# Two q/k pairs between the halves of W_out, and the next batch's V on the ACT queue: a fused attention and hard-swish kernel on one core

## The chip, the cores and the metric

The kernel runs on one core of one Trainium2 chip. The metric is the device time of one execution in microseconds (us); less is better. All times below are in us unless they say otherwise.

## What is computed

Causal attention with a window of 64 positions (8 batches, 8 heads, 576 positions, head size 64), then a two-layer feed-forward block over the 4608 resulting rows. Inputs and output are float32.

```python
scores = q @ k.T / sqrt(64)                      # per batch and head
mask = (i - j >= 0) & (i - j < 64)
attn = softmax(where(mask, scores, -1e9))
x = (attn @ v) put together to [4608, 512]
h = x @ w_in                                     # [512, 2048]
g = h * clip(h + 3, 0, 6) / 6
out = g @ w_out                                  # [2048, 512]
```

## The kernel before

The feed-forward block works on nine blocks of 512 rows, T = 0 to 8. For each block, `s1(T)` multiplies with W_in (64 matmuls of 512 columns, tile `ps`, L769); ACT makes relu(h/6 + 1/2) of every two blocks of 128 columns (`relu`, tile `t`, L778), and DVE limits that to 1 and multiplies it with h (`gT`, L781). Then `s2(T)` multiplies with W_out (64 matmuls, tile `acc`, L813) and ACT copies each of the four accumulators out (`osb`, L830), which SP stores. Between the matmuls of `s2(T)` stand the units of attention of batch T + 1: T (transposes on TensorE, L570, for batches 0 and 1 only), S (scores, L601 or L650, followed by an exponential on ACT and a mask on DVE, L621 or L660), PV (attention times V, L674, L687 and L692, followed by a normalisation on DVE, L712 and L715) and X (transposes of the result, L739; from batch 2 on a DMA transpose, L722). Each unit serves one of four groups of two heads. Three pairs of PSUM banks serve all of `ps`; two accumulators serve `acc`.

The kernel builds its own order: a planner (`Plan`) holds a heap of operations with assumed durations, and every engine's instructions come out in the order of the planned starts. At run time each engine and each queue works strictly in that order and waits on semaphores.

Loads arrive in staging tiles (six of `st`, three of `tl` for the short last piece) and are cast to bf16. Batches 0 and 1 load q and k as four pairs, one for each group (L337, tile `runs`), whose casts go to DVE, ACT or POOL, whichever the planner finds free first. Batches from 2 on load q and k "naturally" in five pieces each (L463, tile `nat`), cast by POOL, and transposed by one DMA each on SP (L442, tile `QKT`). V comes in five pieces. For batches 0 and 1 it is on SP (L420, L362); from batch 2 on, `stream_v` issues it on ACT's queue (L389), and POOL makes up to three casts of each piece, one into `V` and two into a copy shifted by 64 rows, which lies in the memory of `runs`. The first full-width weights are four blocks of W_in (L493; the first in two halves) and four of W_out (L508), cast by POOL.

SP takes the loads in the order that `load_items` yields. For batch 0 and batch 1 `MERGE` says how q/k pairs (p) and pieces of V (v) alternate:

```python
MERGE = ('ppppvvvppvpvpvvvvv', "ppppppvpvpvvv")
```

so that the order is batch 0, all of W_in, all of W_out, batch 1 with V among the last pairs, and then q and k of batch 2, 3 and so on. `stream_v(b)` is put into the plan after q and k of batch b; its issues depend on `("pv", b - 2, NG - 1)` and `("issued", b, 0)`, that is, on the last PV of batch b - 2 and on the issue of the q transpose of batch b.

All DMAs issued by SP and ACT take one of eight semaphores in turn, in the order of the program. Each issue waits until the DMA that last used its semaphore, eight issues before, has landed.

`s2(0)` takes its 64 matmuls in an order of its own, since W_out is still arriving: block columns 0 to 11 for the first two groups of 128 rows, then 12 to 15 for these, then the other two groups.

Of the kernel before, what the change touches and what calls it, by code (L numbers as in the profile page):

```python
# [21 lines left out]
NQT = 1  # L22
NPT = 3
VGAP = 1.8
VRATE = 150
NXP = 2
NEG = -30000.0
QK_ENG = ((('DVE', 'ACT'), ('ACT',), ('ACT',), ('ACT',)), (("DVE", "ACT"),) * 4)
MERGE = ('ppppvvvppvpvpvvvvv', "ppppppvpvpvvv")
ORDER = (('T', 0), ('T', 1), ('S0', 0), ('S1', 0), ('S1', 1), ('T', 2), ('S0', 1), ('PV', 0), ('S1', 2), ('T', 3), ('S0', 2), ('PV', 1), ('S1', 3), ('PV', 2), ('S0', 3), ('X', 0), ('PV', 3), ('X', 2), ('X', 1), ('X', 3))  # L30
X_ENG = ((('DVE',), ('DVE', 'ACT'), ('DVE',), ('DVE', 'ACT')), (("DVE", "ACT"),) * 4)
NWARM = 11
# [71 lines left out]
def kernel(  # L104
# [10 lines left out]
    P = nc.NUM_PARTITIONS  # L115
    B, H, S, D = q.shape
    DM, FF = moe_w_in.shape
    NT = B * S
    NG = H // 2
# [5 lines left out]
    NFC = FF // P  # L125
# [171 lines left out]

    def load_items():

        for b in range(B):  # L300
            if b < NR6:
                ps, vs = load_pairs(b), load_v_halves(b) if b == 0 else load_v(b)
                for c in MERGE[b]:
                    yield next(ps if c == "p" else vs)
            else:
                yield from load_nat(b)
            if b == 0:
                yield from load_w()

    def casts(key, land, pieces):  # L310

# [14 lines left out]
    def load_pairs(b):  # L326

        for gg in range(0, NG, 2):
            tiles = {}
            deps = [stage_slot([("cast", b, i, gg), ("cast", b, i, gg + 1)]) for i in range(2)]  # L330
            for g in (gg, gg + 1):
                for i, src in enumerate((q, k)):
                    def go(s, g=g, i=i, src=src, tiles=tiles):
                        if i not in tiles:
                            tiles[i] = stage.tile([P, 2, R * D], F32, name="st", tag="st")
                        st = tiles[i][:, g % 2, :]
                        nc.sync.dma_start(  # L337
                            out=st,
                            in_=src[b, 2 * g : 2 * g + 2].rearrange("h (p j) d -> (h p) (j d)", j=R),
                        )  # L340
                        fr, land = moved(s, 295, 385 if b else 330)
                        casts(("cast", b, i, g), land, [
                            (("DVE", "ACT", "POOL"), runs[i][b * NG + g][:], st.rearrange("p (j d) -> p j d", j=R), R * D)])
                        return fr
                    yield b, deps[i], go
# [27 lines left out]
    def stream_v(b):  # L373

        V, W = V_ring[b % 2], W_ring[b % 2]
        tiles = {}
        deps = stage_slot([("cast", b, 2, i) for i in range(KB - 1)]) + (("pv", b - 2, NG - 1), ("issued", b, 0))
        tdeps = tail_slot([("cast", b, 2, KB - 1)])

        def issue(kb):  # L380
            ss = min(P, S - kb * P)
            def fn(s):
                if kb == 0:
                    tiles["t"] = stage.tile([P, 4, H * D], F32, name="st", tag="st")
                    tiles["l"] = tails.tile([P, H * D], F32, name="tl", tag="tl")
                if kb == KB - 1:
                    pl.mark(("vgo", b), s)
                st = tiles["l"][:ss, :] if kb == KB - 1 else tiles["t"][:, kb, :]
                nc.scalar.dma_start(  # L389
                    out=st.rearrange("p (h d) -> p h d", h=H),  # L390
                    in_=v[b, :, kb * P : kb * P + ss, :].rearrange("h s d -> s h d"),
                )
                dma["v"] = max(dma["v"], s) + 262 * ss / P / VRATE
                land = dma["v"] + 2.7
                sv = st.rearrange("p (g h d) -> p g h d", g=NG, h=2)
                todo = [(("POOL",), W[D:P, :, kb, :, 0:D], sv[0:D], H * D)]
                if ss == P:
                    todo.append((("POOL",), V[:, :, kb, :, 0:D], sv, H * D))
                    todo.append((("POOL",), W[0:D, :, kb + 1, :, 0:D], sv[D:P], H * D))
                casts(("cast", b, 2, kb), land, todo)  # L400
                if kb < KB - 1:
                    pl.op("ACT", s + VGAP, 0.45, issue(kb + 1))
            return fn
        pl.op("ACT", 0.0, 0.45, issue(0), deps=deps + tdeps)

# [23 lines left out]
                yield b, deps + tdeps if kb == KB - 1 else deps, go  # L429

    def load_nat(b):
        for i, src in enumerate((q, k)):
            T = {"left": KB}
            n = natural[i]
            deps = stage_slot([("cast", b, i, j) for j in range(KB - 1)])
            if b > NR6:
                deps += (("vgo", b - 1),)
            if b > NR6:
                deps += (("tr", b - 1, i),)
            def tr(t, i=i, n=n):  # L440
                def fn(s):
                    nc.sync.dma_start_transpose(  # L442
                        out=QK_tiles[b % NQT][:, i * NG : (i + 1) * NG, :].rearrange("d g (k t) -> d (g k) t", t=P),
                        in_=n[:].rearrange("p g k d -> p (g k d)"),
                    )
                    fr, land = moved(s, 655, 230)
                    pl.free["SP"] = fr
                    pl.mark(("issued", b, i), s)
                    return land
                d = (("S", b - NQT, NG - 1),) if b >= NQT else ()  # L450
                if b > 2:
                    d += (("s1", b - 1),)
                pl.op("SP", t, 0.1, fn, ("tr", b, i), deps=d)
            for kb in range(KB):
                ss = min(P, S - kb * P)
                def go(s, i=i, src=src, kb=kb, ss=ss, T=T, n=n, tr=tr):
                    if kb == 0:
                        T["t"] = stage.tile([P, 4, H * D], F32, name="st", tag="st")
                    if kb == KB - 1:
                        st = tails.tile([P, H * D], F32, name="tl", tag="tl")[:ss, :]  # L460
                    else:
                        st = T["t"][:, kb, :]
                    nc.sync.dma_start(  # L463
                        out=st.rearrange("p (h d) -> p h d", h=H),
                        in_=src[b, :, kb * P : kb * P + ss, :].rearrange("h s d -> s h d"),
                    )
                    fr, land = moved(s, 262 * ss / P, 205)
                    def done(t):
                        T["left"] -= 1
                        if not T["left"]:  # L470
                            tr(t)
                    pl.op("POOL", land, 0.61,
                          cast_op("POOL", n[:ss, :, kb, :], st.rearrange("p (g d) -> p g d", g=NG)),
                          ("cast", b, i, kb), done)
                    return fr
                yield b, deps + tail_slot([("cast", b, i, kb)]) if kb == KB - 1 else deps, go
        stream_v(b)

    WC = FF // 4

# [308 lines left out]
    def s2(T, side):  # L789

        side = list(side)
        if T == 0:
            order = [(ts, fc) for f0 in (0, 12) for ts in (0, 1) for fc in range(f0, 12 if f0 == 0 else NFC)]
            order += [(ts, fc) for ts in (2, 3) for fc in range(NFC)]
        else:
            order = [(ts, fc) for ts in range(TB // P) for fc in range(NFC)]
        accs = {}
        for n, (ts, fc) in enumerate(order):
            while side and side[0][0] <= n:
                at_, f, b, g = side[0]  # L800
                if b < NR6 and not ready(f, b, g):
                    break
                side.pop(0)
                unit(f, b, g)
            if fc == 0:
                nst = T * 4 + ts
                if nst >= 2:
                    pl.wait(("acc", (nst - 2) // 4, (nst - 2) % 4))
                accs[ts] = acc_pool.tile([P, DM], F32, name="acc", tag="acc")[:]
            pl.wait(("g", T, fc // 2))  # L810
            if T == 0:
                pl.wait(("wout", fc // 4, (fc % 4) // 2))
            nc.tensor.matmul(  # L813
                accs[ts], lhsT=gT[:, fc, ts * P : (ts + 1) * P], rhs=wout16[:, fc, :],
                start=(fc == 0), stop=(fc == NFC - 1),
            )
            pl.pe(0.216)
            if fc == NFC - 1:
                finish(T, ts, accs[ts])
        for _, f, b, g in side:  # L820
            unit(f, b, g)
# [96 lines left out]
```

## Time and profile before

| | us |
|---|---|
| median of 6 runs | 315.13 |
| lowest and highest run | 313.12, 316.87 |
| the profiled execution | 316.87 |
| its span in the profile | 315.1 |

The profiled execution is the highest of the six. Some of its places, in us from the span's start:

| what | from | to |
|---|---|---|
| s1(0) on TensorE | 22.36 | 36.53 |
| s2(0) with the attention of batch 1 | 36.53 | 63.23 |
| s1(1) | 63.23 | 77.04 |
| first scores of batch 2 | 78.29 | |
| V of batch 2, issues on ACT | 60.38 | 68.91 |
| q and k transposes of batch 2, issues on SP | 66.35 | 76.79 |
| s2(2) starts | 110.88 | |

"Engine A waited for B" in these views is inferred from semaphores. A DMA's issue and its landing are two times: the queue is busy with the issue, the data is there at the landing. The granted TensorE clock was 0.998 of full speed.

### The profile page before, as it was taken

The page shows a single profiled execution, that of the slowest core. Times are in us where ns is not written, and L with a number is a line of the kernel's source. Part 1 is how long each engine was busy: PE and PEld are TensorE (multiplying, and loading weights), DVE is VectorE, ACT ScalarE, POOL GpSimd, SP SyncE. Part 2 cuts the span into 40 slices and gives each one's busy share as a digit, 9 for nine tenths or more (in the row PEclk, how much of TensorE's full clock was granted, in tenths as well). Part 3 has the DMA queues.
Part 4 walks back from the last instruction along what each step waited for, and adds up shares of the span by engine and source line. Part 5 has one row for each costly group of instructions (what it writes and reads, how often), then busy time and mean ns, then how long its engine had stood idle before and what let it go on. Part 6 is the DMA issues. An engine that isn't in the chain of part 4 may idle for free.

```text
span 315.1 us, 6662 instructions
## 1 busy us (share of the span) xinstructions
PE 301.2 (96%) x2771; PEld 152.6 (48%) x2771; DVE 160.7 (51%) x205; ACT 154.1 (49%) x194; POOL 118.5 (38%) x187
## 2 busy tenths in 40 slices
PE   7889888999998999999998999999999999999995
PEld 3454344644543444785543444444575444444442
DVE  5486746847633574276426661666166616404600
ACT  4855527556614562366335723672367236315611
POOL 3166747548444463256324642375361000000000
PEclk9999999999999999999999999999999999999999
DMA  7999999999999999999999999999990620010011
GB/s 217 233 334 387 386 306 216 234 213 212 217 176 239 247 211 178 190 248 190 177 206 229 205 184 225 193 198 179 238 247 2 132 89 0 33 69 33 1 67 67
DMA packets 153342, 58.37 MB, mean 185 GB/s; under 512 B 142048, under 2 KB 143072, under 8 KB 153312
## 3 DMA queue, kind: packets, MB, share of 16 engines
q1 hardware_dynamic: 125184, 50.87, 75.9%
q10 hardware_dynamic: 28128, 7.08, 12.5%
q8 instruction: 21, 0.34, 0.5%
q14 instruction: 9, 0.07, 0.1%
HBM read 36.70 MB, written 9.44 MB: 146 GB/s over the span
## 4 chain that ended last, share of the span: by engine, by line
PE 65%; DMA 25%; SPq 3%; POOL 2%; ACT 1%; issue 1%; DVE 1%; ACTq 0%; POOLq 0%
PE acc L813 34%; PE ps L769 24%; DMA QKT<-nat 7%; DMA st<-in_v_dram 6%; DMA st<-in_moe_w_out_dram 4%; DMA st<-in_k_dram 4%; DMA st<-in_moe_w_in_dram 3%; PE ps L674 3%; PE ps L650 3%; SPq L337 2%; SPq L420 1%; POOL runs L281 1%; DVE gT L781 1%; ACT t L778 1%; ACT pT L610 0%
## 5 line engine op out<-in xcount | busy, mean ns | idle before, releaser
L781 DVE SCALAR_TENSOR_TENSOR gT<-t,ps 128x1024 bf16<-128x1024 bf16 x72 | 87.6, 1221 | 104.9 <-ACT t L778 104.9
L813 PE MATMUL acc<-wout,gT 128*128 128x512 bf16 x576 | 134.7, 380 | 1.9 <-POOL wout L281 1.5
L769 PE MATMUL ps<-xT,win 128*128 128x512 bf16 (+4 forms) x704 | 126.9, 340 | 2.8 <-DVE gT L781 1.6
L778 ACT ACTIVATE t<-ps,half 128x1024 bf16<-128x1024 f32 x72 | 79.9, 1114 | 54.2 <-PE ps L769 51.9
L769 PEld LDWEIGHTS <-win 128*128 128x128 bf16 x704 | 65.2, 98 | 62.9 <-issue 3.6
L813 PEld LDWEIGHTS <-gT 128*128 128x128 bf16 x576 | 52.5, 98 | 60.6 <-issue 2.4
L830 ACT COPY osb<-acc 128x512 f32<-128x512 f32 x36 | 21.0, 589 | 74.3 <-PE acc L813 71.4
L281 POOL CAST runs<-st 64x512 bf16<-64x512 f32 (+1 forms) x49 | 31.1, 635 | 58.1 <-DMA st<-in_v_dram 55.9
L281 POOL CAST nat<-st 128x512 bf16<-128x512 f32 x48 | 32.7, 689 | 24.9 <-DMA st<-in_k_dram 13.4
L656 ACT ACTIVATE pT<-ps 128x640 bf16<-128x640 f32 (+1 forms) x48 | 28.7, 650 | 9.8 <-PE ps L650 9.8
L715 DVE TENSOR_TENSOR opg<-ps,rec 128x640 bf16<-128x640 f32 x32 | 26.4, 824 | 1.1
L660 DVE TENSOR_TENSOR pT<-pT,mask 128x1152 bf16<-128x1152 bf16 x24 | 18.5, 773 | 6.0 <-ACT pT L656 6.0
L281 POOL CAST V<-st 128x512 bf16<-128x512 f32 (+1 forms) x30 | 18.2, 607 | 8.2 <-DMA st<-in_v_dram 6.6
L610 ACT ACTIVATE pT<-ps 128x768 bf16<-128x768 f32 x16 | 12.6, 819 | 3.7 <-PE ps L601 3.7
L278 DVE CAST runs<-st 128x576 bf16<-128x576 f32 x15 | 7.6, 512 | 10.9 <-DMA st<-in_q_dram 7.5
L650 PEld LDWEIGHTS <-QKT 64*128 64x128 bf16 x432 | 7.6, 95 | 10.4 <-issue 10.4
L712 DVE RECIPROCAL rec<-ps 128x10 f32<-128x10 f32 x32 | 7.0, 217 | 10.9 <-PE ps L674 9.6
L280 ACT COPY QKT<-ps 128x1152 bf16<-128x1152 bf16 x6 | 6.8, 1129 | 11.3 <-PE ps L570 11.3
L674 PEld LDWEIGHTS <-pT 128*64 128x64 bf16 x480 | 9.5, 111 | 5.7 <-DVE opg L715 2.5
L674 PE MATMUL ps<-runs,pT 128*64 128x65 bf16 x288 | 12.2, 197 | 0.0
L674 PE MATMUL ps<-V,pT 128*64 128x65 bf16 x192 | 11.3, 198 | 0.0
L281 POOL CAST nat<-tl 64x512 bf16<-64x512 f32 x12 | 8.2, 680 | 7.4 <-DMA tl<-in_k_dram 4.9
(59 smaller groups left out, 122.6 us busy)
## 6 DMA issues: line engine op xcount, KB each, us to landing
out_dram<-osb SPq DMA_DIRECT2D x36, 256.0 KB, 3.7
st<-in_q_dram SPq DMA_DIRECT2D x24, 256.0 KB, 6.1
st<-in_k_dram SPq DMA_DIRECT2D x24, 256.0 KB, 6.0
st<-in_v_dram ACTq DMA_DIRECT2D x24, 256.0 KB, 5.3
st<-in_moe_w_out_dram SPq DMA_DIRECT2D x4, 1024.0 KB, 16.0
st<-in_moe_w_in_dram SPq DMA_DIRECT2D x3, 1024.0 KB, 11.4
st<-in_q_dram SPq DMA_DIRECT2D x8, 288.0 KB, 6.0
st<-in_k_dram SPq DMA_DIRECT2D x8, 288.0 KB, 6.7
```

The source lines that it names most:

```text
L281: return lambda s: nc.gpsimd.tensor_copy(out=out_ap, in_=in_ap) and None
L610: nc.scalar.activation(out=pT[:, :, kbs[0] : kbs[0] + 2, 0:QW], in_=st[:, :, 0 : 2 * QW].rearrange("p h (k w) -> p h k w", k=2), func=EXP, ...
L650: nc.tensor.matmul(st[:, h, c : c + D], lhsT=kwin(b, g, i, h), rhs=QT[h * D : (h + 1) * D, i * D : (i + 1) * D], start=True, stop=True,)
L656: nc.scalar.activation(out=pT[:, :, i0 * D : i1 * D], in_=st[:, :, 0 : (i1 - i0) * D], func=EXP, scale=scale,)
L660: pl.op("DVE", t, 0.8, lambda s: nc.vector.tensor_tensor(out=pT.rearrange("p h (i w) -> p (h i) w", w=D), in0=pT.rearrange("p h (i w) -> p ...
L674: nc.tensor.matmul(o[odd * D : (odd + 1) * D, h, m * VW : (m + 1) * VW], lhsT=pT[:, h, i * D : (i + 1) * D], rhs=(V if i % 2 else W)[:, g, ...
L715: nc.vector.tensor_tensor(out=opg[:].rearrange("p k h d -> p h k d"), in0=ov[:, :, :, 0:D], in1=rec[:].unsqueeze(3).to_broadcast([P, 2, KB ...
L769: nc.tensor.matmul(hT[:, j, dst : dst + w], lhsT=win16[:, g, (2 * c + j) * P : (2 * c + j + 1) * P], rhs=xT[:, g, src : src + w], start=(g ...
L778: nc.scalar.activation(out=t1[:], in_=hT[:], func=RELU, bias=half[:], scale=1.0 / 6.0)
L781: nc.vector.scalar_tensor_tensor(out=gT[:, 2 * c : 2 * c + 2, :], in0=cell["t"][:], scalar=1.0, in1=hT[:], op0=MIN, op1=MULT,)
L813: nc.tensor.matmul(accs[ts], lhsT=gT[:, fc, ts * P : (ts + 1) * P], rhs=wout16[:, fc, :], start=(fc == 0), stop=(fc == NFC - 1),)
L830: nc.scalar.copy(out=osb[:], in_=acc)
```

## The change

`MERGE` is replaced by one sequence over all the loads up to batch 1, in which w stands for a weight block, and capitals for batch 1:

```diff
-MERGE = ('ppppvvvppvpvpvvvvv', "ppppppvpvpvvv")
+VGAP2 = 2.5
+SEQ = "ppppvvvppvpvpvvvvv" "wwwwwww" "PPPPww" "PPPPVVVVV"
...
-        for b in range(B):
-            if b < NR6:
-                ps, vs = load_pairs(b), load_v_halves(b) if b == 0 else load_v(b)
-                for c in MERGE[b]:
-                    yield next(ps if c == "p" else vs)
-            else:
-                yield from load_nat(b)
-            if b == 0:
-                yield from load_w()
+        src = {"p": load_pairs(0), "v": load_v_halves(0), "w": load_w(), "P": load_pairs(1), "V": load_v(1)}
+        for c in SEQ:
+            yield next(src[c])
+        for b in range(NR6, B):
+            yield from load_nat(b)
```

The first two q/k pairs of batch 1 (q0, k0, q1, k1) now stand after the second block of W_out; then come the other two blocks, the other two pairs, and V of batch 1 in one run. For batch 2 (`NR6` is 2), `stream_v` goes into the plan ahead of q and k, its first issue depends only on the cast of batch 1's first piece of V, its issues are planned 2.5 apart instead of 1.8, and q and k of batch 2 wait in the plan until its first issue has been placed:

```diff
-        deps = stage_slot([...]) + (("pv", b - 2, NG - 1), ("issued", b, 0))
+        deps = stage_slot([...]) + ((("pv", b - 2, NG - 1), ("issued", b, 0)) if b > NR6 else (("cast", 1, 2, 0),))
...
-                if kb == KB - 1:
+                if kb == (0 if b == NR6 else KB - 1):
                     pl.mark(("vgo", b), s)
...
-                    pl.op("ACT", s + VGAP, 0.45, issue(kb + 1))
+                    pl.op("ACT", s + (VGAP2 if b == NR6 else VGAP), 0.45, issue(kb + 1))
...
     def load_nat(b):
+        if b == NR6:
+            stream_v(b)
...
-            if b > NR6:
-                deps += (("vgo", b - 1),)
+            deps += (("vgo", max(b - 1, NR6)),)
...
-        stream_v(b)
+        if b > NR6:
+            stream_v(b)
```

`s2(0)` takes its first two groups of rows in three steps instead of two:

```diff
-            order = [(ts, fc) for f0 in (0, 12) for ts in (0, 1) for fc in range(f0, 12 if f0 == 0 else NFC)]
+            order = [(ts, fc) for f0 in (0, 8, 12) for ts in (0, 1) for fc in range(f0, 8 if f0 == 0 else f0 + 4)]
```

What follows for the order of the instructions: on TensorE the transposes of the first group of batch 1 stand ahead of the first matmul of s2(0), and those of the second three matmuls later, where 22 and 25 matmuls stood ahead of them; 43 matmuls instead of 48 stand ahead of the first PV of batch 1. On DVE and ACT, casts of q0 and k0 stand between the last `gT` and `relu` of s1(0). On ACT the five issues of V of batch 2 stand among the copies and exponentials of s2(0), the last behind the fourth `osb` copy. On POOL the casts of V of batch 2 alternate with those of q and k of batch 2. From batch 3 on, the order of every engine is as it was.

More of the change, by code (lines that the diff above doesn't have):

```diff
@@ L376, in stream_v @@
         tiles = {}
-        deps = stage_slot([("cast", b, 2, i) for i in range(KB - 1)]) + (("pv", b - 2, NG - 1), ("issued", b, 0))
+        deps = stage_slot([("cast", b, 2, i) for i in range(KB - 1)]) + ((("pv", b - 2, NG - 1), ("issued", b, 0)) if b > NR6 else (("cast", 1, 2, 0),))
         tdeps = tail_slot([("cast", b, 2, KB - 1)])
```

## The prediction

> **What bounds the kernel now.** I read the engine shares first, then the chain that ended last, then TensorE's timeline for its idle gaps, and only in those gaps the other queues.
>
> ```profile
> PE 301.2 (96%) x2771; PEld 152.6 (48%) x2771; DVE 160.7 (51%) x205; ACT 154.1 (49%) x194; POOL 118.5 (38%) x187
> ```
>
> TensorE is busy for 96%, so only its gaps can be won. Its blocks repeat: s2(3), s2(5), s2(6) and s2(7) start at 142.69, 206.78, 238.48 and 269.97, so an undisturbed round takes 31.5 to 31.7. The rounds that this change touches are longer. TensorE's timeline says where (start, us, what, idle before it and what ended that):
>
> ```profile
> 36.53 2.06 PE L813 MATMUL acc<-wout,gT 128*128 128x512 bf16 x8
> 39.73 0.59 PE L813 MATMUL acc<-wout,gT 128*128 128x512 bf16 x2 [1.13 <-POOL wout L281]
> 49.43 0.38 PE L813 MATMUL acc<-wout,gT 128*128 128x512 bf16 x1 [0.41 <-ACT osb L830]
> 51.32 0.75 PE L570 MATMUL ps<-ident,runs 64*64 64x64 bf16 x35 [0.59 <-POOL runs L281]
> 63.23 13.98 PE L769 MATMUL ps<-xT,win 128*128 128x512 bf16 x64
> ...
> 78.29 0.44 PE L650 MATMUL ps<-QKT 64*128 64x64 bf16 x18 [0.23 <-DMA QKT<-nat]
> ...
> 96.67 10.15 PE L769 MATMUL ps<-xT,win 128*128 128x512 bf16 x46 [1.06 <-DMA xT<-opg]
> 107.43 3.61 PE L769 MATMUL ps<-xT,win 128*128 128x512 bf16 x16 [0.61 <-DVE gT L781]
> ```
>
> s2(0) with batch 1's attention runs from 36.53 to 63.23, 26.7. Its work is 64 matmuls of 0.216 (13.8) and the units T 0.75, S 0.46, PV 0.53, X 0.29, four of each (8.1): some 22. So about 4.7 is waiting for loads. A second place is 78.29, where the first scores of batch 2 start as its k transpose lands. The chain of waits names that path:
>
> ```profile
> 27.17 14.12 DMA st<-in_moe_w_out_dram
> ...
> 72.98 5.17 DMA QKT<-nat
> 78.16 0.14 issue
> 78.29 0.44 PE ps L650 x18
> ```
>
> **Loads, part one: pairs between the halves.** No byte is added. In the trace's landings a weight block is 2.71 behind the one before it and a pair's tile 0.75 (42.04, 42.80, 43.56, 44.32): one saturated queue in order. The second weight block lands at 35.87 as now. Then q0, k0, q1, k1 land at 36.6, 37.4, 38.1, 38.9 (now 42.0 to 44.3), the last two blocks at 41.6 and 44.3 (now 38.6 and 41.3), and the other two pairs at 45.1 to 47.3. V of batch 1 comes last in one run: 4.5 pieces at 1.0 to 1.55 (its own and batch 2's pieces now) give 51.8 to 54.3; I take 53.2, against 53.55 now, since the sum of bytes is the same. The split of s2(0) at block columns 8 and 12 adds no matmul, only lets the first 16 run on two weight blocks. POOL loses the cast of k3 (49.76, 1.50) to DVE, and with it the 0.59 idle at 51.32.
>
> **TensorE through s2(0).** Row by row: DVE has the q0 cast between gT number 4 and 5, so gT 5, which now runs at 34.43, waits for 36.6 and ends at 38.4; ACT has the k0 cast before relu 6. The transposes T0 now stand in front of s2's first matmul and need a PSUM slot of gT 5: they start at 38.4, not 36.53 (1.9 idle). T1 needs gT 6, delayed with relu 6 to 40.6 (0.9 idle). Then 21 matmuls follow without a wait, since the third and fourth weight blocks are cast by 43.7 and 46.4. T2, S1, T3 find their casts done. The third accumulator waits for the first's copy, which stands behind S1's exponentials on ACT (0.9; now 0.41). So TensorE reaches PV0 at 53.7 with 43 matmuls done; now it is at 55.61 with 48, which is 54.5 with 43. PV0 needs V's last piece cast: POOL has two casts, two pairs of fills and three casts there, ending at 54.1 to 54.8. The rest (21 matmuls, 4 PV, one S, 4 X: 8.3) ends at 62.5, bounds 61.9 and 63.0, against 63.23: a gain of 0.7, bounds 1.3 and 0.2. The 4.7 of waiting is moved to the front more than removed.
>
> **V of batch 2 on ACT.** Five issues stand between s2(0)'s copies and exponentials; each takes 0.37 to 0.43 at the least now (2.0 in all, one took 1.30). They come off the place behind X1 (60.38 to 68.91) and so leave s1(1)'s relu. The exponentials of S2 move by 0.4 and PV2 needs them 2 later: nothing on the path. An issue also waits for the landing of the DMA eight before it on the common ring of semaphores, and everything behind it on ACT waits too. The five wait for k2, the first V piece, V's last piece, the second q piece of batch 2 and q's last piece; all but the last have landed by then. The last (q's tail, about 62) stands in front of relu 0, wanted at 64.2: hidden, with 1 to 2 to spare. SP gains waits of the same kind: k's first piece behind the second V piece, the third store behind the third, the q transpose behind the fourth.
>
> **What is late next: the k transpose of batch 2.** At 62.5 + 13.81 (s1(1)) + 0.86 (four matmuls) TensorE wants it at 77.2. It lands 5.17 after its start, if that stays. Three things release the start. DMA: from 53.2 on, 13.5 pieces of 0.262 MB and three stores, 4.32 MB, come ahead of k's last piece, of which V's last two pieces are new. The windows show what rate to use:
>
> ```profile
> 56.00:64.00 8.00, 7.97 (x115) 5.00 (x112) 6.13 (x11) 4.43 (x8) 4.34 (x7) 1.00 1.08 240
> 64.00:72.00 8.00, 8.00 (x39) 3.63 (x37) 4.18 (x4) 4.46 (x4) 3.98 (x7) 1.00 1.31 196
> ```
>
> The last number is GB/s: 240 with nearly all on SP's queue, 196 with both queues. That bounds the landing at 71.2 and 75.2. I take 71.2, since 64 to 72 also holds a wait of SP (k's tail issued only at 65.63, when a V piece had landed). POOL: 23 casts stand between V of batch 1 and k's last piece, at 0.683 from start to start 15.7, from 54.7 on, 1.2 of it spent waiting for the first V piece (issued at 51.3, landing 5.3 later) and 0.6 beside a mask:
>
> ```profile
> 49.76 1.50 POOL L281 CAST runs<-st 128x576 bf16<-128x576 f32 x1 [0.27 <-DMA st<-in_k_dram]
> 53.81 1.23 POOL L281 CAST V<-tl 64x512 bf16<-64x512 f32 x1
> 70.82 0.61 POOL L281 CAST nat<-tl 64x512 bf16<-64x512 f32 x1 [2.41 <-DMA tl<-in_k_dram]
> ```
>
> Sum 72.2, against 71.43 now. SP: the q transpose can start at about 65, as now (66.35), takes 5.43, a store 0.5: 71. So POOL is last, the start is 72.3 (now 72.98), landing 77.5, scores at 77.6 against 78.29: 0.7 gained, of which nothing is lost later. Batch 3's loads start when SP is done with that transpose, now 1.45 ahead of the scores and then about as much, so the gaps of 1.06 and 0.61 stay. I take 0.6.
>
> **Two rules.** The first two rows above are casts beside VectorE's mask (1.15 each): 1.50 and 1.23 instead of 0.61. The Trainium skill, SBUF — State Buffer, "Who interferes with whom", says that a VectorE instruction with two SBUF inputs and a GpSimd one that reads SBUF block each other for the whole instruction. By that rule two masks would cost POOL up to 2.3 and the gain would be gone; by the rows it is 0.6 to 0.9 each. The Trainium skill, DMA: Bandwidth & Descriptors, "Issuing engines are not separate DMA queues", speaks against the second half of the change: transfers issued by several engines share the same 16 DMA engines, and only issue time is saved. By that rule V beside q and k brings no byte earlier; the windows of 240 and 196 say the same or worse.
>
> **Rivals.** (A) Faster: casts and pieces flow at their best. Pieces 1.0 apart, as q's of batch 2 are now (54.50, 55.53, 56.49), put k's last landing at 68.8, and POOL without waits ends at 70.4. The transpose starts by 70.5, the scores at 77.1, and SP is 3 ahead instead of 1.45, so the 1.06 before s1(2) goes as well: 1.2 + 1.06 = 2.3 gained, 312.8. For it: 244 GB/s moved from 53.6 to 65.4. Against it: POOL's order, V and nat in turn, waits for the later of two queues each time. (B) Slower: two queues at 196 GB/s. k's last piece at 75.2, cast 75.9, transpose landing 81.2, scores 2.9 later than now, and SP's lead no better: 318.0. It decides against the change from below 225 GB/s, and by more than 0.5% from below 208. For it: the window of 196 and 203 at 80 to 88. (C) ACT stands before relu 0 because q's tail lands after 65: each later us beyond 1.7 is paid; 2 more gives 317.1. That the change does nothing is no rival: the order of all five engines moves.
>
> **How the numbers follow.** The profiled execution took 316.87 (span 315.1 and 1.77 around it), 1.74 above the median of six, 315.13. Minus 0.6: 316.3 for such an execution, 314.5 for the median. The forecast's own range, from its bounds of 1.2 gained and 0.3 lost, is 313.9 to 315.4. What a measurement can tell from no change is about 0.5%, 1.6 us. Chances: forecast 0.50 (0.44 within, 0.05 faster, 0.01 slower), A 0.25 (0.23 faster), B 0.21 (0.20 slower), C 0.04. Faster 0.28, within 0.47, slower 0.25. The range 312.5 to 317.2 takes in A and the lower part of B.
>
> **What would show it.** Right: T0 at 38.4 with 1.9 idle before it, s1(1) at 62.5, scores of batch 2 still released by the transpose, at 77.6, and the gap of 1.06 kept. Wrong: scores released by TensorE itself (A), k's tail landing after 74 (B), relu 0 of s1(1) behind a DMA issue (C), or V of batch 1 in after 55.

## The result, and the profile after

The changed kernel takes 315.01 us (median of 37 runs, 313.30 to 316.89), the kernel before, run beside it, 314.37 (74 runs, 311.85 to 319.49). The ratio is 1.0032, with a 95% interval of 1.0018 to 1.0045: 0.3% slower, about 1.0 us. The ratio leaves out slow runs, those over 1.5% above the fastest of their kernel, of which before has nine and the changed kernel none; over all runs the means are 315.12 and 314.52, 0.6 us apart. The result lies inside the range and within the 0.5%, but on the other side of zero than the 0.6 us that were forecast. The execution of before that the prediction argued from, 316.87, was the fifth longest of the 74; two more traces of it and two more of the changed kernel were therefore taken, and they matter below.

The engine shares of the changed kernel, from its page (profiled execution 315.14, span 313.4, clock 1.000):

```profile
PE 299.8 (96%) x2771; PEld 152.6 (49%) x2771; DVE 161.1 (51%) x204; ACT 155.8 (50%) x196; POOL 117.1 (37%) x186
```

TensorE is as full as before. Its timeline (start, busy, line, idle before it and what ended that):

```profile
37.65 0.76 PE L569 MATMUL ps<-ident,runs 64*64 64x64 bf16 x36 [1.78 <-DVE gT L780]
39.73 0.76 PE L569 MATMUL ps<-ident,runs 64*64 64x64 bf16 x36 [0.58 <-DVE gT L780]
49.88 0.38 PE L812 MATMUL acc<-wout,gT 128*128 128x512 bf16 x1 [0.41 <-ACT osb L829]
54.34 0.19 PE L686 MATMUL ps<-V,pT 128*128 128x65 bf16 x1 [1.26 <-POOL V L282]
63.93 13.98 PE L768 MATMUL ps<-xT,win 128*128 128x512 bf16 x64
78.70 0.44 PE L649 MATMUL ps<-QKT 64*128 64x64 bf16 x18
96.91 13.56 PE L768 MATMUL ps<-xT,win 128*128 128x512 bf16 x62 [0.89 <-DMA xT<-opg]
```

The waits for W_out and for the casts of the pairs are gone, and new ones stand at the head of s2(0) (1.78 and 0.58) and before PV0 (1.26, 0.34 and 0.60). s2(0) took 28.1 us, 1.5 more than in the trace before (26.5), and the first scores of batch 2 came when TensorE was ready for them, not when k's transpose landed. Read from these two traces alone, the loss lies in s2(0). The second trace of the same changed kernel (r3) says otherwise:

```profile
53.13 0.19 PE L686 MATMUL ps<-V,pT 128*128 128x65 bf16 x1 [0.85 <-POOL V L282]
78.18 0.44 PE L649 MATMUL ps<-QKT 64*128 64x64 bf16 x18 [2.01 <-DMA QKT<-nat]
96.03 13.72 PE L768 MATMUL ps<-xT,win 128*128 128x512 bf16 x61 [0.54 <-DMA xT<-opg]
```

Here s2(0) takes 25.7, and TensorE waits 2.01 for k's transpose of batch 2. Both traces reach the scores of batch 2 at the same distance from s1(0): 56.8 and 56.5. What both have in common is the late transpose: it landed at 56.47 and 56.35.

The traces of all kernels but e5, side by side; the labels are explained with the experiments below. All positions are us from the start of s1(0), since the start itself varies from 20.95 to 22.55. "V ahead" counts the pieces of V of batch 2 that landed before k's last piece; QKT is the landing of k's transpose; S(2) and S(3) in the table are the first scores of batches 2 and 3 (in the recorded expectations S(3) can also be the fourth unit of scores of batch 1). From S(3) to the end, every trace of a kernel within 1% of before takes 202.1 to 202.8, but the first one of before (203.3): beyond S(3) nothing changes. The ratio is that of the timed runs.

| kernel, trace | V(1) last | s2(0) takes | V ahead | k last | QKT | S(2) | s1(2) takes | S(3) | time to before |
|---|---|---|---|---|---|---|---|---|---|
| before | 31.2 | 26.5 | 3 | 48.4 | 55.8 | 55.9 | 16.0 | 89.5 | |
| before (r1) | 30.2 | 26.1 | 3 | 47.4 | 55.2 | 55.3 | 16.8 | 89.7 | |
| before (r2) | 29.9 | 25.5 | 3 | 46.2 | 53.7 | 54.2 | 14.6 | 86.3 | |
| changed | 33.1 | 28.1 | 5 | 49.6 | 56.5 | 56.8 | 15.0 | 89.4 | 1.0032 [1.0018, 1.0045] |
| changed (r3) | 29.6 | 25.7 | 5 | 49.2 | 56.4 | 56.5 | 14.9 | 88.9 | |
| changed (x0) | 30.0 | 26.1 | 5 | 49.1 | 56.2 | 56.4 | 15.1 | 89.0 | 1.0027 [1.0004, 1.0050] |
| e1, loads only | 29.7 | 25.7 | 4 | 47.8 | 55.5 | 55.7 | 15.7 | 88.9 | 1.0026 [1.0000, 1.0053] |
| e2, V early only | 32.4 | 27.9 | 5 | 50.0 | 56.5 | 57.6 | 14.1 | 89.1 | 1.0017 [0.9992, 1.0043] |
| e3b, V behind V(1) | 30.0 | 25.8 | 3 | 46.3 | 55.3 | 55.4 | 15.3 | 88.2 | 1.0000 [0.9972, 1.0029] |
| e3d, V behind batch 1's last scores | 29.2 | 25.6 | 3 | 46.1 | 54.5 | 54.6 | 15.1 | 87.3 | 1.0020 [0.9989, 1.0050] |
| e3d again (r4) | 30.1 | 25.7 | 3 | 46.3 | 55.0 | 55.1 | 15.3 | 88.0 | |
| e6, V 5.0 apart | 30.6 | 25.5 | 3 | 47.0 | 55.2 | 55.3 | 15.0 | 87.8 | 1.0014 [0.9978, 1.0049] |
| e7, before, V behind k | 30.1 | 26.0 | 0 | 43.1 | 54.1 | 54.7 | 15.0 | 88.0 | 1.0006 [0.9974, 1.0038] |
| y1, V's casts behind k's | 32.3 | 28.8 | 5 | 49.3 | 55.6 | 57.5 | 14.0 | 89.0 | 1.0011 [0.9981, 1.0041] |
| x3, changed, xT first | 31.2 | 26.2 | 5 | 49.0 | 55.9 | 56.1 | 14.4 | 88.0 | 0.9993 [0.9965, 1.0022] |
| y2, y1 and xT first | 30.2 | 26.4 | 5 | 49.7 | 56.2 | 56.3 | 14.6 | 88.4 | 0.9999 [0.9972, 1.0026] |
| x2, before, xT first | 30.2 | 25.9 | 3 | 46.7 | 54.1 | 54.6 | 14.0 | 86.1 | 0.9986 [0.9960, 1.0011] |
| x1, V late, xT first | 30.0 | 25.9 | 2 | 45.5 | 55.8 | 55.9 | 14.1 | 87.5 | 0.9962 [0.9940, 0.9985] |
| x1 again (z1) | 29.8 | 25.5 | 3 | 45.9 | 54.5 | 54.6 | 14.0 | 86.1 | 0.9974 [0.9946, 1.0001] |

The account by means of three traces each: S(2) comes 1.4 later in the changed kernel (56.55 against 55.15), s1(2) is 0.8 shorter (14.99 against 15.83), S(3) is 0.6 later (89.06 against 88.49). The times say 0.6 (medians) to 1.0 (ratio). Single traces of one kernel differ by up to 1.7 at S(2) and 3.3 at S(3), so only what repeats in several traces is used below; the 0.6 at S(3) does not show by itself.

### The profile page after: what moved, and what is told of

Read it like the earlier page. It is cut to its first block, busy times and chain, and to the rows that moved or that the text cites. A ratio compares the mean times of both kernels' runs of the same rounds, so it can differ in the third digit from the quotient of the medians.

```text
span 313.4 us, 6667 instructions
## 1 busy us (share of the span) xinstructions
PE 299.8 (96%) x2771; PEld 152.6 (49%) x2771; DVE 161.1 (51%) x204; ACT 155.8 (50%) x196; POOL 117.1 (37%) x186
## 4 chain that ended last, share of the span: by engine, by line
PE 78%; DMA 11%; SPq 6%; POOL 2%; issue 1%; DVE 0%; ACT 0%; ACTq 0%; POOLq 0%
PE acc L812 36%; PE ps L768 35%; DMA st<-in_moe_w_out_dram 5%; PE ps L673 3%; SPq L359 3%; PE ps L649 3%; DMA tl<-in_v_dram 2%; DMA st<-in_v_dram 2%; DMA xT<-opg 2%; SPq L334 2%; SPq L417 1%; POOL wout L282 1%; SPq L721 0%; POOL V L282 0%; PE ps L686 0%
## 5 line engine op out<-in xcount | busy, mean ns | idle before, releaser
L780 DVE SCALAR_TENSOR_TENSOR gT<-t,ps 128x1024 bf16<-128x1024 bf16 x72 | 87.8, 1221 | 100.5 <-ACT t L777 100.5
L282 POOL CAST runs<-st 64x512 bf16<-64x512 f32 x48 | 30.4, 634 | 56.6 <-DMA st<-in_v_dram 48.1
L282 POOL CAST nat<-st 128x512 bf16<-128x512 f32 x48 | 30.7, 643 | 33.1 <-DMA st<-in_q_dram 16.6
L714 DVE TENSOR_TENSOR opg<-ps,rec 128x640 bf16<-128x640 f32 x32 | 26.4, 824 | 1.1
L659 DVE TENSOR_TENSOR pT<-pT,mask 128x1152 bf16<-128x1152 bf16 x24 | 19.9, 830 | 5.8 <-ACT pT L655 5.8
L282 POOL CAST V<-st 128x512 bf16<-128x512 f32 (+1 forms) x30 | 19.8, 662 | 6.6 <-DMA st<-in_v_dram 5.0
L282 POOL CAST wout<-st 128x1024 bf16<-128x1024 f32 x8 | 9.3, 1191 | 5.6 <-DMA st<-in_moe_w_out_dram 5.6
L281 ACT COPY QKT<-ps 128x1152 bf16<-128x1152 bf16 x7 | 7.9, 1127 | 5.9 <-PE ps L569 5.9
```

Of the source, the lines that this page charges most:

```text
L282: return lambda s: nc.gpsimd.tensor_copy(out=out_ap, in_=in_ap) and None
L659: pl.op("DVE", t, 0.8, lambda s: nc.vector.tensor_tensor(out=pT.rearrange("p h (i w) -> p (h i) w", w=D), in0=pT.rearrange("p h (i w) -> p ...
L714: nc.vector.tensor_tensor(out=opg[:].rearrange("p k h d -> p h k d"), in0=ov[:, :, :, 0:D], in1=rec[:].unsqueeze(3).to_broadcast([P, 2, KB ...
L780: nc.vector.scalar_tensor_tensor(out=gT[:, 2 * c : 2 * c + 2, :], in0=cell["t"][:], scalar=1.0, in1=hT[:], op0=MIN, op1=MULT,)
```

## The experiments

**The parts by themselves, and V of batch 2 later.** e1 is the changed kernel with V of batch 2 as before; e2 is the kernel before with only `stream_v` moved; e3b and e3d have the change's loads, but the first issue of V behind the last cast of V of batch 1 (e3b), or behind the exponential of batch 1's fourth and last scores (e3d), and do not hold q and k for it. The theory then was that V of batch 2 cuts into V of batch 1.

```diff
 e1: deps of stream_v, its place, its distance, and vgo as before; SEQ and the order of s2(0) as changed
 e2: deps of stream_v, its place, VGAP2 and vgo as changed; MERGE and the order of s2(0) as before
 e3b and e3d, on the changed kernel:
-            deps += (("vgo", max(b - 1, NR6)),)
+            if b > NR6:
+                deps += (("vgo", b - 1),)
 e3b: -(("cast", 1, 2, 0),)   +(("cast", 1, 2, KB - 1),)
 e3d: -(("cast", 1, 2, 0),)   +(("exp", 1, 3, 1),)
```

> The new load order and the three-step order of s2(0), with V of batch 2 issued as in the kernel before. Theory (V of batch 2 cuts in: its first piece, issued on ACT at 48.0, takes 1.3 of transfer time ahead of the last two pieces of V of batch 1, for which the first PV waits 2.2): the last piece of V of batch 1 lands at about 53.5 instead of 55.0, the waits inside the first PV fall from 2.2 to below 1, and the ratio to the kernel before is 0.998 to 1.000. Rival (V of batch 1 in one run is what is slow: its first piece lands 2.6 after the last pair, where 1.0 to 1.5 was reckoned): the last piece stays at 55, the waits at 2, the ratio at 1.003. Second rival (the transposes in front of s2(0) and the 1.8 + 0.6 of idle at its head cost the time): ratio 1.003 with V in time.

> The load order of the kernel before, with V of batch 2 issued early on ACT. Theory (V of batch 2 cuts in): some piece of V of batch 1 lands 1 or more later than in the kernel before (53.55), the first PV waits, the ratio is 1.002 to 1.005. Rivals (the run of V, or the head of s2(0)): neither is in this kernel, so the ratio is 1.000, or below by what the earlier q and k transposes bring.

> The changed kernel with the first issue of V of batch 2 placed behind the exponentials of the third scores (planned after the last cast of V of batch 1 instead of the first), and q and k of batch 2 not held for it in the plan. Theory: the issue goes out at about 51 instead of 48, when two pieces of V of batch 1 are still on their way; it shares with them, so the last piece lands at 53.5 to 54.3, the waits in the first PV are about 1, the ratio 0.998 to 1.001, between the changed kernel (1.003) and e3d. Rivals: 1.003, with the waits unchanged.

> The changed kernel with the first issue of V of batch 2 placed behind the exponentials of the fourth scores, and q and k of batch 2 not held for it. Theory: the issue goes out at about 57, behind all of V of batch 1, whose last piece lands at about 53.5; waits in the first PV below 1; s1(1) starts 1.2 to 1.5 earlier than in the changed kernel; the ratio is 0.997 to 1.000. Rivals: the last piece at 55, ratio 1.003.

All four times lie within 0.3% of before; they don't tell the parts apart. The theory had e1 and e3d at 1.000 or below: they came at 1.0026 and 1.0020, so the times don't bear it out. The traces say more. In the six traces with the new load order and V of batch 2 late (e1, e3b, e3d, r4, x1, z1), s2(0) takes 25.5 to 25.9, 0.3 less than the mean of before (26.0, single traces 25.5 to 26.5): that is the most that the load order can be said to gain. Where V is early and its first piece landed ahead of V of batch 1's last one (changed, e2, x3, y1, e6), V(1)'s last came at 30.6 to 33.1 in place of 29.2 to 30.2 (31.2 in the first trace of before, though), and s2(0) took 27.9 to 28.8 in three of the five. Where V was early and did not get ahead (r3, x0, y2), s2(0) took 25.7 to 26.4. So the cut is there, but in some executions only, and it is not what both kinds share. TensorE's timeline of e3d, with both V's out of each other's way:

```profile
53.37 0.19 PE L687 MATMUL ps<-V,pT 128*128 128x65 bf16 x1 [0.88 <-POOL V L282]
76.63 0.44 PE L650 MATMUL ps<-QKT 64*128 64x64 bf16 x18 [0.21 <-DMA QKT<-nat]
```

PV0 still waits 0.88 for V's casts, but S(2) all but meets its transpose.

**The spread of one kernel.** The kernel before twice more, the changed one, and e3d once more, one execution each.

> The kernel before, unchanged, for a second trace of it: the trace shown so far is of an execution of 316.87 us, 2.5 us over the median of 314.37, and from s1(4) to s1(5) it takes 32.6 us where every trace of the other five kernels takes 31.5 to 31.8. If that execution is typical up to the first scores of batch 3, these come 89.5 us after the start of s1(0) here too, and s2(0) takes 26.5 us. If it was late by chance there as well, they come at 88 to 89, and what the traces of the changed kernels seemed to gain (0.6 us for the load order alone, 2.2 us with V of batch 2 after S(3)) shrinks to what the times show, nothing.

> The kernel before once more, for the spread between two executions: if the first scores of batch 3 lie within 0.3 us of the other trace's, counted from the start of s1(0), positions in one trace can be compared to that; if they differ by a microsecond, they can't, and only lengths that repeat may be used.

> The changed kernel, unchanged, for a second trace. Theory (V of batch 2 cuts in): V of batch 1's last piece lands again 1.3 to 1.5 us later behind V2 than without V of batch 2, and s2(0) is again longer than before. What it leaves open is the first piece of V, 2.56 us behind k's last piece in the trace, where the load order alone shows 0.95: it landed only 1.2 us after V of batch 2's first issue. If that repeats, it belongs to the change and s2(0) is 28.1 us again; if it was chance, the piece lands about 1.0 behind k's last, and s2(0) takes 26.3 to 27.0.

> Load order of the change, with V of batch 2 started only behind the exponential of S(3) and q and k not held for it, once more. Its first trace was of its fastest execution (313.14 against a median of 314.92). If s2(0) takes 25.6 us and the first scores of batch 3 come 87.2 us after the start of s1(0) again, the gain is there in every execution and the median was raised by something later or earlier; if they come at 88 to 89, the trace was a lucky one.

The two traces of before, r1 first (r2's s1(2) has one wait of 0.49, its S(2) at 76.00 none):

```profile
76.93 0.44 PE L650 MATMUL ps<-QKT 64*128 64x64 bf16 x18 [0.45 <-DMA QKT<-nat]
95.37 1.02 PE L769 MATMUL ps<-xT,win 128*128 128x512 bf16 x4 [1.12 <-DMA xT<-opg]
97.79 12.68 PE L769 MATMUL ps<-xT,win 128*128 128x512 bf16 x57 [1.40 <-DMA xT<-opg]
```

```profile
76.00 0.44 PE L650 MATMUL ps<-QKT 64*128 64x64 bf16 x18
94.66 12.68 PE L769 MATMUL ps<-xT,win 128*128 128x512 bf16 x57 [0.49 <-DMA xT<-opg]
```

With one program, S(2) lies between 54.2 and 55.9, and the wait for xT in s1(2) between 0.5 and 2.5: the second option of r2's expectation. r1 by itself fits neither option of its own: S(3) comes at 89.7, as in the first trace, but s2(0) takes 26.1. In the trace that the prediction used, S(2) was the latest of the three. For r3 the expectation's second case holds: V's first piece landed 0.99 behind k's last pair (2.56 in the first trace, cause not found), and s2(0) took 25.7, less than the 26.3 that were expected at the least. e3d's second trace (r4) reaches S(3) at 88.0, so 0.7 of its 87.3 did not repeat.

**Where V stands among q and k.** k's last piece of batch 2 lands at 49.0 to 50.0 in all seven traces with five pieces of V ahead, at 47.8 with four, at 45.9 to 48.4 with three. It is not only that SP issues k's last load later: with three ahead it lands at 46.1 (e3d) and 46.3 (r4) though it was issued at 38.1 and 39.3, and at 47.4 (r1) and 46.2 (r2) where it was issued at 42.0 and 41.0. e6 keeps V early but spreads it; e5 and e7 put it behind k's transpose in the plan.

```diff
 e6: -VGAP2 = 2.5   +VGAP2 = 5.0
 e5, on e3d: -(("exp", 1, 3, 1),)   +(("issued", b, 1),)
 e7, on the kernel before: -("issued", b, 0)   +("issued", b, 1 if b == NR6 else 0)
```

> The changed kernel with one number changed, the planned distance between V of batch 2's issues on ACT, 5.0 us in place of 2.5. Theory (V of batch 2 goes ahead of k): three or four pieces of V land before k's last piece in place of five, so that lands at 46.2 to 47.8 from the start of s1(0) in place of 49.2 and 49.6, QKT at 54.7 to 55.6 in place of 56.4, and the time falls by 0.7 to 1.5 us, to that of before or less. Rival (the second queue by itself slows q and k, however V is spaced, as they start behind V's first issue in both): k's last piece lands at 49 again and the time is the changed kernel's.

> Load order of the change, V of batch 2 started only when k's transpose of batch 2 is issued, q and k not held for it. Theory (V of batch 2 goes ahead of k): in nine traces k's last piece of batch 2 lands, counted from the start of s1(0), at 49.2 to 50.0 with all five pieces of V landed before it, 47.8 with four, 46.1 to 46.3 with three under the new load order, so 1.5 us for each; with none or one ahead it lands at 42 to 44, QKT at 49 to 52, and the first scores of batch 2 come at 54.3 to 54.5, when TensorE has done s1(1), with no wait for QKT. V of batch 2 then lands some 10 us later than in the trace before and PV(2) may wait for it; if it does, the time is above before. Rival (transposes and POOL's casts set QKT, not the loads): k's last piece may land early, but QKT still lands at 54.5 or later.

> The kernel before with one condition changed: V of batch 2 waits for k's transpose to be placed, not q's. Theory: before, three pieces of V land ahead of k's last piece (46.2 to 48.4 from the start of s1(0)); with none to two ahead k's last lands 1.5 to 4.5 us earlier, QKT at 52 to 54 in place of 53.7 to 55.8, and the first scores of batch 2 come when TensorE is ready, 0.2 to 0.5 us earlier than in the traces of before that wait for QKT. Time between 1 us below and 0.5 above before, above if PV(2) waits for V. Rival (V's place does not matter, the sum of the bytes does): QKT lands where it did.

e6: three pieces ahead, k's last at 47.0, QKT at 55.2, S(3) at 87.8. One number moved them by 2.3, 1.2 and 1.3 us from the means of the changed kernel, whose three traces lie within 0.6 of each other at all three places: as the theory said, in one trace. Its ratio, 1.0014, lies between the changed kernel's and 1 and excludes neither. TensorE's line of S(2):

```profile
77.00 0.44 PE L649 MATMUL ps<-QKT 64*128 64x64 bf16 x18 [0.93 <-DMA QKT<-nat]
```

e7: none ahead, k's last at 43.1, 3.1 to 5.3 us earlier than before, but QKT only at 54.1, and the time does not move. Here its rival was right in part: k's transpose ran beside V's pieces and took 9.5 from its start to its landing, where the traces of before show 5.2 to 6.1, so with fewer than three pieces ahead nothing more was gained at QKT. (x1, with two ahead and k's last at 45.5, has QKT only at 55.8.) e5 goes too far: 324.95 us, ratio 1.0283 [1.0199, 1.0367]. In its trace (granted clock 0.979) V of batch 2 lands at 50.8 to 62.3 and PV of batch 2 waits for its casts, 6.2 us in five waits, of which the longest are

```profile
85.30 0.22 PE L674 MATMUL ps<-runs,pT 128*64 128x65 bf16 x1 [2.33 <-POOL runs L282]
88.01 0.22 PE L674 MATMUL ps<-runs,pT 128*64 128x65 bf16 x1 [1.82 <-POOL runs L282]
90.05 0.27 PE L674 MATMUL ps<-runs,pT 128*64 128x65 bf16 x3 [1.14 <-POOL runs L282]
```

**The road to the end: SP's queue.** Behind QKT's transposes SP has the ten loads of batch 3, then the four transposes to xT. x3, x2 and x1 put the last two loads of k of batch 3 behind those transposes, on the changed kernel, on before, and on e3d; x0 is the changed kernel beside them.

```diff
-                yield b, deps + tail_slot([("cast", b, i, kb)]) if kb == KB - 1 else deps, go
+                more = (("x", 2, 3),) if b == 3 and i == 1 and kb >= 3 else ()
+                yield b, (deps + tail_slot([("cast", b, i, kb)]) if kb == KB - 1 else deps) + more, go
```

> The changed kernel, for a third trace and times beside the three that follow. Theory: five pieces of V land before k's last piece of batch 2, k's last at 49.2 to 49.6 from the start of s1(0), QKT at 56.3 to 56.5, the first scores of batch 3 at 88.8 to 89.4; time 0.5 to 1.4 us above before.

> The changed kernel with the last two loads of k of batch 3 (one and a half pieces, some 1.7 us of transfer) put behind the four xT transposes of batch 2 on SP. Theory (SP's queue carries the loss to s1(2)): the xT transposes land 1.5 to 2 us earlier, the waits in s1(2), 1.1 and 0.9 us in the two traces, are gone, and the first scores of batch 3 come at 87.8 to 88.2 from the start of s1(0); time 0.7 to 1.2 us below the changed kernel's, the time of before. QKT of batch 3 lands 2 to 3 us later, which had 3 to 4 us to spare. Rival (the loss is all in the first scores of batch 2): s1(2) has little to give and the time falls by under 0.3 us; or QKT of batch 3 becomes late and it rises.

> The kernel before with the same two loads of k of batch 3 behind the xT transposes. Theory: its s1(2) loses its waits (2.1, 2.9 and 0.7 us in three traces) and starts the scores of batch 3 at 86 to 87.2 from s1(0); time 0.7 to 2 us below before. If the time does not move, the wait for xT is no part of what sets the end.

> Load order of the change, V of batch 2 behind the exponential of S(3), q and k not held for it, and the two loads of k of batch 3 behind the xT transposes: both roads of the loss taken away. Theory: k's last of batch 2 at 46.1 to 46.3, first scores of batch 2 at 54.5 to 55.2, no wait in s1(2), first scores of batch 3 at 86 to 86.8 from s1(0); time 1 to 2 us below before, the lowest of all. Rival: a new wait takes it back, QKT of batch 3 first.

SP's timeline, x0 first and then x1 (the first line of each is k's load ahead of the transposes):

```profile
85.30 1.21 SPq L461 DMA_DIRECT2D tl<-in_k_dram  x1
86.62 0.56 SPq L832 DMA_DIRECT2D out_dram<-osb  x1
87.28 3.94 SPq L721 DMA_TRANSPOSE xT<-opg  x3
```

```profile
80.02 3.34 SPq L462 DMA_DIRECT2D st<-in_k_dram  x3
83.45 1.11 SPq L834 DMA_DIRECT2D out_dram<-osb  x1
84.66 5.00 SPq L723 DMA_TRANSPOSE xT<-opg  x3
```

The transposes start 2.6 earlier in x1, 3.3 counted from s1(0). In x3 s1(2) loses 0.7 and S(3) is 1.0 earlier than in x0 (the expectation said 87.8 to 88.2: 88.0); the time goes from 1.0027 to 0.9993. x0 and x3 ran beside each other, twelve runs each: their means are 315.04 and 313.79, and the spread of the runs gives the difference as 1.25 ± 0.75 us (95%). That wait for xT is thus worth about a microsecond of the changed kernel's time. In x2 s1(2) has no wait left and S(3) comes at 86.1, yet the time, 0.9986, is not clear of 1: r2's own 86.3 shows that before reaches this by itself in some executions. x1 is the one version clearly below before, 0.9962 [0.9940, 0.9985], 312.77 us against 314.20. Its trace does not show why: S(2) at 55.9 and S(3) at 87.5 are later than expected. But x1 and x3 differ only in V of batch 2 (late, and q and k not held for it, against early), and ran beside each other too: 312.98 against 313.79 in the mean, 0.8 ± 0.8. z1 and y2 below, the same pair but for the order of some casts, give 0.6 ± 0.7. Together these are the nearest thing to a price of V's early place in the time, 0.7 ± 0.5; in the first series e3b is 0.9 below e2, but e3d is level with it.

**POOL's order.** x0's chain of waits went through POOL's casts from 62.5 on, V's among k's, with two gaps of 0.33 and 0.74 and from 67.5 on without one (the "issue" lines of 0.04 to 0.06 and some others left out):

```profile
62.49 0.61 POOL nat L282
...
68.21 0.62 POOL runs L282
68.89 0.62 POOL V L282
69.57 0.62 POOL runs L282
70.25 0.62 POOL nat L282
70.93 0.62 POOL runs L282
...
71.60 0.62 POOL nat L282
72.24 4.94 DMA QKT<-nat
```

y1 puts the casts of V's last three pieces behind k's, with the loads untouched; y2 does so on x3; z1 is x1 again.

```diff
-                casts(("cast", b, 2, kb), land, todo)
+                casts(("cast", b, 2, kb), land, todo, (("cast", b, 1, KB - 1),) if b == NR6 and kb >= 2 else ())
```

> The changed kernel with its loads untouched; on POOL the casts of the third, fourth and last piece of V of batch 2 (eight casts, 0.68 us each from start to start, of which seven stood ahead of k's last) are put behind k's last cast. Theory (POOL's order of casts): k's last is cast 0.7 us after it lands in place of 1.9 to 2.3, so its transpose lands 1.2 to 1.6 us earlier, at 54.7 to 55.2 from the start of s1(0) in place of 56.2 to 56.5, and the first scores of batch 2 come with it; the time falls by 0.3 to 1 us, to that of before. Rival (the loads): k's last piece lands at 49.1 as before, and q's transpose on SP or the landing itself then sets QKT, which moves by under 0.5 us.

> y1, and the last two loads of k of batch 3 behind the xT transposes of batch 2. Theory: the gains of y1 (up to 1 us) and of x3 (1 us) add up, the first scores of batch 3 come at 86.5 to 87.2 from the start of s1(0) in place of 89.1, and the time is 0.5 to 1.2 us below before. If y1 gains nothing, this is x3 again (0.9993 of before).

> x1 again, the load order of the change with V of batch 2 behind S(3) and xT first: if its 0.9962 was no chance it comes out between 0.994 and 0.9985 again, 0.5 to 1.9 us below before.

The theory of POOL's order failed for the larger part. In y1 k's last is cast as it lands,

```profile
71.90 0.61 POOL L282 CAST nat<-tl 64x512 bf16<-64x512 f32 x1 [0.87 <-DMA tl<-in_k_dram]
```

and SP is right behind it: k's last load issued at 67.18, q's transpose from 67.89 to 72.02, a store, k's transpose at 73.23. QKT lands at 55.6 and, in y2, 56.2: 0.7 and 0.1 earlier than the changed kernel's 56.3, not 1.2 to 1.6. What is left is SP's row, behind k's late last load, as y1's rival said (which allowed under 0.5); POOL's row of casts in x0's chain ran beside SP's row and hid it. y1's time is not distinguishable from before or from the changed kernel, and its s2(0) was one of those hit by the cut. z1 gives 0.9974 [0.9946, 1.0001] for x1: the expected range, and its interval just touches 1.

## Why the prediction was wrong

- **The reference point.** The sum was made against positions in one trace, the slowest run of six. Against that trace, S(2) of the changed kernel was to move from 55.9 to 55.2; the mean of three traces of before is 55.15. 0.8 of the 2.1 us between forecast (0.7 earlier) and measurement (1.4 later) is this. The median of six runs was high as well, 315.13 where 74 runs give 314.37: that the changed kernel's 315.01 falls into the forecast's own range of 313.9 to 315.4 is luck.
- **The release of k's transpose: the step that failed.** The sum had POOL release it last, at 72.2, with SP ready at 71 and k's last piece landed at 71.2, and so started it at 72.3. Counted from s1(0), as below, that is 49.9, with the landing at 55.1; it started at 51.3 to 51.5 and landed at 56.2 to 56.5. All three terms took it that q and k of batch 2 come no later for V's lead. They did: q's last piece landed at 41.5 to 41.8 (36.8 to 38.2 before), and k's last load was issued at 44.3 to 44.9 (41.0 to 43.3 before). The three terms one by one:
- **The loads.** "240 with nearly all on SP's queue, 196 with both queues ... I take 71.2." The windows from V(1)'s last landing to k's last, in r3 and then in e3d (the last number is GB/s):

```profile
51.30:70.84 19.54, 18.53 (x169) 10.21 (x171) 12.01 (x16) 9.07 (x13) 14.61 (x22) 1.00 1.16 215
51.23:68.11 16.88, 15.89 (x157) 8.95 (x158) 9.64 (x14) 8.22 (x13) 9.60 (x15) 1.00 1.23 229
```

  Taken from 30.0 on to k's last piece in all three traces of each kernel, it is 215 to 223 GB/s and 4.1 to 4.4 MB (rate times length) for the changed one, 223 to 228 GB/s and 3.7 to 4.1 MB for before. So of the 2.0 by which k's last came later in the mean, the bytes ahead of it make some 1.4, and the lower rate at most the rest (e6, with three pieces ahead again, has 216 too). The 240 was too high for this stretch, and the trace of before could show it: 224 from 53.55 to 70.77. Rival B, which decides against the change from below 225, thus had the direction, but not its rate of 196, and its sign (k's tail after 74) did not come: k's last landed at 49.1 to 49.6, where the forecast's 71.2 is 48.8 and B's 75.2 is 52.8. This term alone was out by only 0.3 to 0.8. The Trainium skill, DMA: Bandwidth & Descriptors, "Issuing engines are not separate DMA queues", which the prediction weighed, agrees with these rows: on ACT's queue V brought nothing faster and only changed its place in the order, to ahead of k.
- **POOL's sum.** 23 casts, 1.2 of waiting and 0.6 of masks gave 17.5 from V's last cast to k's. In r3 it was 20.0 (53.07 to 73.09): the waits inside were 4.0, for q's late last piece above all. With the cast 1.5 later than the sum had it, and 5.0 for the transpose where 5.2 was foreseen, QKT came 1.2 after the 55.1 of the forecast. (The two casts beside a mask that the prediction sets against the rule of blocking do not speak against it: they began 0.17 and 0.39 into masks of 1.15, and were 0.89 and 0.62 longer than 0.61, where 0.98 and 0.76 of the mask were left.)
- **SP's row.** "The q transpose can start at about 65, as now" is 42.6; it started at 45.0 to 45.6, since k's last load stands ahead of it. r3's rows:

```profile
66.00 0.61 SPq L461 DMA_DIRECT2D tl<-in_k_dram  x1
66.71 4.31 SPq L440 DMA_TRANSPOSE QKT<-nat  x1
71.15 0.49 SPq L832 DMA_DIRECT2D out_dram<-osb  x1
73.12 2.94 SPq L440 DMA_TRANSPOSE QKT<-nat  x1
```

  So SP was free at 50.0 to 50.7 instead of 48.6, and in y1, where POOL was done with k by then, k's transpose started at 50.7. A better order on POOL would have mended only a part.
- **V of batch 2's first issue.** "Issued at 51.3", behind the first copy of s2(0) on ACT. It went at 25.4 to 26.1 from s1(0), not 28.9, ahead of that copy; in some executions it thus came ahead of V of batch 1's last pieces.
- **s2(0): right.** Idle of 1.9 and 0.9 at its head was 1.1 to 1.8 and 0.6; s1(1) was due 40.1 after s1(0) and came at 39.6 and 40.1 where V did not cut in, 42.0 where it did. But the gain of 0.7 was measured from the late trace; from the mean of before it is 0.3 at the most, and the cut takes it away in part of the executions.
- **"The gaps of 1.06 and 0.61 stay": right in size, wrong in meaning.** s1(2) is 0.9 to 1.1 longer than its 13.98 without waits after, 0.7 to 2.8 before. It waits for xT behind SP's loads, so a later S(2) has less to wait for: 0.8 of the 1.4 came back there, in the means. Rival A did not occur, nor C: s1(1) ran its 13.98 without a wait. The sign that was named for A, scores of batch 2 released by TensorE itself, was there in the first trace, but because TensorE was late and not because the transpose was early; the sign that V of batch 1 comes in "after 55" was there too, at 55.0, in that trace alone.

What stays open: why V's first piece of batch 1 was 1.6 late in the first trace; how much of k's delay is V's bytes and how much SP's waits on the ring of eight semaphores, whose places V's issues also take (no run holds one and moves the other); and whether the traces account for the time to better than half a microsecond, since e3d reaches S(3) 0.5 to 1.2 before the mean of before and its time does not show it. That V's early place makes k's transpose late is shown by the traces; that this is the whole of the 0.6 to 1.0 us is not.

## What to carry to other kernels

When the queues are full, as they were here (215 to 229 GB/s in all the windows above), an early transfer is paid for by whichever other lands later: before moving a load forward, ask which one it passes and which of the two is needed first. Here q and k of batch 2 were needed before V, and each piece of V moved ahead of k pushed k's last back by 1.1 to 1.5 us: under the new load order it landed at 43.7 with none ahead (e5), at 46.3 in the mean with three, at 49.3 with five. And take a second trace of the unchanged kernel before subtracting positions of a single one: here two executions of one program differed, 3.3 us at S(3), by more than three times the effect that was measured.

## What the runs showed of the hardware that was not expected

A DMA in ACT's program did not wait for the instructions ahead of it to run. ACT's timeline of the changed kernel; the program has the first of the two copies of the last line ahead of the issue:

```profile
48.02 0.43 ACTq L386 DMA_DIRECT2D st<-in_v_dram  x1
48.36 0.82 ACT L609 ACTIVATE pT<-ps 128x768 bf16<-128x768 f32 x1
49.05 0.30 ACT L615 ACTIVATE pT<-ps 128x128 bf16<-128x128 f32 x1
49.21 1.11 ACT L829 COPY osb<-acc 128x512 f32<-128x512 f32 x2
```

The issue went out 1.2 us ahead of a copy that stands before it, and in r3 too (47.10 against 48.29). It was also ahead of the cast of V of batch 1's first piece, which the plan names as its condition, and which POOL began only at 49.23: such a condition orders the program, it is no wait at run time. The Trainium skill has the reason: Perfetto Trace Analysis, "DVE / Act Engine Instruction (TENSOR_ADD, Activation, etc)", says that the sequencer takes the next instruction once the last is pushed into a queue. These rows agree with it.
